# Moving the q, k transposes to the crossbar DMA and making x the stationary operand of the sequence mixer

## The chip, the cores and the metric

The kernel runs on one core of one Trainium2 chip. The metric is the device time of one execution in microseconds (us). Some executions are slower at a lower granted TensorE clock than others of the same kernel; here it was 4 of the 50 of the experiments' kernels, 1.5 to 2.0% above the mean of their kernel's fast ones, at a clock of 0.962 to 0.974 against 0.968 to 0.982. Such runs are marked slow and are left out of every ratio (the medians below are over all runs). Engines are named as the profile names them: PE is TensorE's matmuls, PEld its weight loads, DVE is VectorE, ACT is ScalarE, POOL is GpSimd, and SP is SyncE, whose queue (SPq) issues DMAs. `L246` is line 246 of the kernel in question.

## The reference, cut to what matters

```python
# q, k, v: (8 batches, 8 heads, 576, 64), s: (8, 8, 576)
scores = q @ k.T / 8 + min(-(cum[i] - cum[j]), 0)   # cum = cumsum(max(s, 0)); causal
x = softmax(scores) @ v                             # heads side by side: (8, 576, 512)
u = x + (x.T @ U @ V).T                             # sequence mixer: U (576, 32), V (32, 576)
out = u + relu(u @ w_ch1) @ w_ch2                   # channel mixer, 512 -> 2048 -> 512
```

## The kernel before

The 64 heads are worked in 32 pairs, four pairs to a batch. The channel mixer of finished batches (`chanmix`, 9 groups) is cut into small steps. They fill TensorE between the steps of the attention (`step_fill`). The parts that the change and the argument touch:

```python
def load_qk(b, h, n):                       # GpSimd's queue, f32 -> bf16
    for dst, src in ((q_t[b], q), (k_t[b], k)):
        nc.gpsimd.dma_start(out=dst[:, ds(h, n), :], in_=...)     # 72 partitions x (8 rows x 64)

def transposes(n):                          # of pair n
    ...                                     # SP: cum rows of the pair into the slot
    for hh in range(2):
        tp = pwork()...                     # a PSUM buffer, one of 4
        for c, src in enumerate((q_t[b], k_t[b])):
            for t2 in range(4):
                nc.tensor.transpose(tp[:, c, t2, :], src[:, h, ds(t2 * 128, 128)], identity[:TP, :TP])
        for par in range(2):
            copy = nc.scalar.copy if n == 0 or (b == 1 and par) else nc.vector.tensor_copy
            copy(dst[:, :, :, :, par], tp[par * D : par * D + D]...)      # into the pair's slot
        yield

def seqmix(b):
    for t in range(5):                      # x U, with U padded to 128 columns as stationary operand
        nc.tensor.matmul(up, lhsT=U_sb[:, t, :], rhs=x_sb[:, :, t, :], ...)      # 512 columns move
    nc.vector.tensor_copy(ux, up)
    yield
    ...                                     # u = x + V-part, 512 columns per matmul

for n in range(PB, NP + 2):                 # the second stage: pairs 4 to 31 (PB = 4, NP = 32)
    b, hp = divmod(n, PB)
    if hp == 0 and 1 < b < B - 1:
        load(b + 1)
    if n + 1 < NP:
        run(transposes(n + 1))              # run(): after each yield, one step of chanmix
    if n < NP:
        run(scores(n))
    ...                                     # seqmix of the batch before, values(n - 1)
in_program_order(tc, traced, [E.Pool, E.PE])
```

Each engine then works through its own list in that order; the traces below show DVE standing 6.36 and 16.72 us at one instruction while a later one is ready.

Names: a slot is the buffer from which a pair's scores are computed (transposed q and k, and the cum rows); there are five, and pair n uses slot n mod 5. `pwork` is a PSUM buffer that matmuls write. `x_sb` is x, the attention's result, as DVE writes it after dividing by the softmax's sum; `ux` is x U; `o_sb` is a piece of the output. `xT` and `u_sd` are transposed by the crossbar DMA (DMA_TRANSPOSE on SP's queue) in this kernel already.

Lines named below: L237 transposes of q and k, L243 copies into the slots, L321 values, L349 x U, L385 and L408 V, L432 and L444 the two channel-mixer matmuls, L98 q, k loads. In the changed kernel the same are L246, L254, L332, L361, L404 and L427, L451 and L463, L97; L342 writes x_sb, L473 writes o_sb, L222 is the new crossbar transpose, which writes `qkT`.

The softmax here doesn't subtract the row's maximum and nothing guards it: scores larger than these inputs give would overflow.

Of the kernel before, what the change touches and what calls it, by code (L numbers as in the profile page):

```python
# [13 lines left out]
BF16 = mybir.dt.bfloat16  # L14
# [25 lines left out]
def kernel(  # L40
# [12 lines left out]
    nc = tc.nc  # L53
    traced = len(nc.cur_bb.bb.instructions)
    E = mybir.EngineType
    B, H, S, D = q.shape
    assert (B, H, S, D) == (8, 8, 576, 64)
    DM = H * D
    FF = 4 * DM
    R = moe_U.shape[1]  # L60
    scale = 1.0 / (D ** 0.5)
    BH = B * H
    NP = BH // 2
    PB = NP // B
    TP, TT = 72, 8
    NG = B * S // 512
    KA = D + 4
    NF = FF // 128
    FT = 2

    consts = ctx.enter_context(tc.tile_pool(name="consts", bufs=1))
    loads = ctx.enter_context(tc.tile_pool(name="loads", bufs=2))
    work = ctx.enter_context(tc.tile_pool(name="work", bufs=2))
    ps_s = ctx.enter_context(tc.tile_pool(name="ps_s", bufs=4, space=bass.MemoryType.PSUM))
    ps_w = ctx.enter_context(tc.tile_pool(name="ps_w", bufs=4, space=bass.MemoryType.PSUM))
# [4 lines left out]
    def pwork():  # L80
        return ps_w.tile([128, 512], FP32, tag="w", name="pwork")
# [5 lines left out]
    rows = s_early[:BH, : 8 * S].rearrange("p (r c s) -> p r c s", r=4, c=2)  # L87
    nc.sync.dma_start(out=s_sb, in_=s.rearrange("b h s -> (b h) s"))

    q_t, k_t = {}, {}  # L90

    def alloc_qk(b):
        q_t[b] = loads.tile([TP, H, TT * D], BF16, tag="q_sd", name="q_sd")
        k_t[b] = loads.tile([TP, H, TT * D], BF16, tag="k_sd", name="k_sd")

    def load_qk(b, h, n):
        for dst, src in ((q_t[b], q), (k_t[b], k)):  # L97
            nc.gpsimd.dma_start(  # L98
                out=dst[:, ds(h, n), :],
                in_=src[b, ds(h, n)].rearrange("h (p t) d -> p h (t d)", p=TP),  # L100
            )

    alloc_qk(0)
    load_qk(0, 0, 2)
    identity = consts.tile([128, 128], BF16)
    make_identity(nc, identity)
# [5 lines left out]
        out=keep,  # L112
        in_=keep,
# [49 lines left out]
    for n in range(PB):  # L163
        for hh in range(2):
            nc.sync.dma_start(
                out=slots[n][D:KA, hh, 0 : 2 * S],
                in_=rows[2 * n + hh : 2 * n + hh + 1].rearrange("n r c s -> n r (c s)"),
            )

    for dst in (q_t[0], k_t[0]):  # L170
        nc.vector.memset(dst[:, 4:8, 0:2], 0.0)
    load_qk(0, 4, 4)
    init_v(nc.vector, v_slots[0])
    for pT in pTs:
        nc.vector.memset(pT[:, :, 1600:], 1.0)
    U_sb = consts.tile([128, 5, 128], BF16)
    nc.vector.memset(U_sb, 0.0)
    V_sb = consts.tile([128, S], BF16)
    nc.vector.memset(V_sb, 0.0)
    rows_hbm = nc.dram_tensor("rows_hbm", (4, BH, 2, S), BF16, kind="Internal").ap()  # L180
    nc.sync.dma_start(
        out=rows_hbm[:, ds(2 * PB, BH - 2 * PB)].rearrange("r n c s -> n r c s"),
        in_=rows[2 * PB :],
    )

    def load_v(b):
# [13 lines left out]
    w1_sb = consts.tile([128, 4, FF], BF16)  # L200
    w2_sb = consts.tile([128, NF, DM], BF16)
    nc.gpsimd.dma_start(
        out=U_sb[:, :4, :R], in_=moe_U[:512].rearrange("(kt kp) r -> kp kt r", kp=128)
    )
    nc.gpsimd.dma_start(out=U_sb[:64, 4, :R], in_=moe_U[512:576])
    nc.gpsimd.dma_start(out=V_sb[:R], in_=moe_V)
    nc.gpsimd.dma_start(out=w1_sb, in_=moe_w_ch1.rearrange("(kt kp) n -> kp kt n", kp=128))
    nc.gpsimd.dma_start(out=w2_sb, in_=moe_w_ch2.rearrange("(kt kp) n -> kp kt n", kp=128))
    alloc_qk(1)
    load_qk(1, 0, H)  # L210
    load_v(1)

    uT_of, x_of, xT_of = {}, {}, {}

    def uT(g):
        if g not in uT_of:
# [1 line left out]
        return uT_of[g]  # L218



    def transposes(n):  # L222
        b, hp = divmod(n, PB)
        slot = slots[n % NSLOT]
        if b > 0:
            nc.sync.dma_start(
                out=slot[D:KA, :, 0 : 2 * S],
                in_=rows_hbm[:, ds(2 * n, 2)].rearrange("r n c s -> r n (c s)"),
            )
        for hh in range(2):  # L230
            h = 2 * hp + hh
            tp = pwork().bitcast(BF16)[:, : 2 * 4 * TP].rearrange(
                "p (c t m) -> p c t m", c=2, t=4
            )
            for c, src in enumerate((q_t[b], k_t[b])):
                for t2 in range(4):
                    nc.tensor.transpose(  # L237
                        tp[:, c, t2, :], src[:, h, ds(t2 * 128, 128)], identity[:TP, :TP]
                    )
            dst = slot[0:D, hh, 0 : 2 * S].rearrange("p (c m t two) -> p c m t two", c=2, t=4, two=2)  # L240
            for par in range(2):
                copy = nc.scalar.copy if n == 0 or (b == 1 and par) else nc.vector.tensor_copy
                copy(  # L243
                    dst[:, :, :, :, par],
                    tp[par * D : par * D + D].rearrange("p c t m -> p c m t"),
                )  # L246
            yield
# [61 lines left out]
    def values(n):  # L309
        b, hp = divmod(n, PB)  # L310
        if hp == 0:
            x_of[b] = work.tile([128, PB, 5, 128], BF16, tag="x_sb", name="x_sb")
            if b >= FT:
                xT_of[b] = work.tile([128, 4, 640], BF16, tag="xT", name="xT", bufs=1)
        x_sb, pT, vt = x_of[b], pTs[n % 2], v_slots[b % 3]
        for hh in range(2):
# [19 lines left out]
            )  # L336
            if hh == 1 and b >= FT:
                nc.sync.dma_start_transpose(
# [5 lines left out]

    def seqmix(b):
        x_sb = x_of.pop(b)
        up = pwork()
        for t in range(5):
            nc.tensor.matmul(  # L349
                up,  # L350
                lhsT=U_sb[:, t, :],
                rhs=x_sb[:, :, t, :],
                start=(t == 0),
                stop=(t == 4),
            )
        ux = work.tile([128, DM], BF16, tag="ux", name="ux")
        nc.vector.tensor_copy(ux, up)  # L357
        yield
        xT = xT_of.pop(b, None)
        cut = 512 - 64 * b  # L360

        def evac(dt, lo, hi, src):

            g, at = (b, 64 * b + lo) if lo < cut else (b + 1, lo - cut)
            dst = uT(g)[:, dt, at : at + hi - lo]
            if xT is not None:
                nc.vector.tensor_tensor(dst, src, xT[:, dt, lo:hi], op=ALU.add)  # L367
            elif b == 0 and type(dt) is int and dt % 2:
                nc.scalar.copy(dst, src)
            else:  # L370
                nc.vector.tensor_copy(dst, src)

        for dt in range(4):
            ut = pwork()
            if xT is None:
                for t in range(4):
                    nc.tensor.matmul(
                        ut[:, ds(t * 128, 128)],
                        lhsT=x_sb[:, dt, t, :],
                        rhs=identity,  # L380
                        start=(t == 0),
                        stop=False,
                        skip_group_check=True,
                    )
            nc.tensor.matmul(  # L385
                ut,
                lhsT=ux[:, ds(dt * 128, 128)],
                rhs=V_sb[:, 0:512],
                start=(xT is not None),
                stop=True,  # L390
                skip_group_check=True,
            )
            evac(dt, 0, cut, ut[:, 0:cut])
            if cut < 512:
                evac(dt, cut, 512, ut[:, cut:512])
            yield
        ut = pwork()[:, 0:256].rearrange("p (a b) -> p a b", a=4)
        for dt in range(4):
            if xT is None:
                nc.tensor.matmul(  # L400
                    ut[:, dt, :],
                    lhsT=x_sb[:, dt, 4, :],
                    rhs=identity[:, :64],
                    start=True,  # L404
                    stop=False,
                    skip_group_check=True,
                )
            nc.tensor.matmul(  # L408
                ut[:, dt, :],
                lhsT=ux[:, ds(dt * 128, 128)],  # L410
                rhs=V_sb[:, 512:S],
                start=(xT is not None),
                stop=True,
                skip_group_check=True,
            )
        evac(slice(0, 4), 512, S, ut)
        yield
# [59 lines left out]
    def run(gen):  # L477
        for _ in gen:
            step_fill()

    def drain(gen):
        for _ in gen:
            pass
# [10 lines left out]
    for n in range(PB):  # L494
        drain(scores(n, 1))
        if n + 2 < PB:
            drain(transposes(n + 2))
        if n > 0:
            drain(values(n - 1))
    drain(values(PB - 1))  # L500
    spin(4, pscore)
    for _ in seqmix(0):
# [2 lines left out]


    def load(b):
        alloc_qk(b)
        load_qk(b, 0, H)
        load_v(b)  # L510

# [3 lines left out]
    fill_with(14)  # L515
    pace[1] = 3
    run(transposes(PB))
    for n in range(PB, NP + 2):
        b, hp = divmod(n, PB)
        if hp == 0 and 1 < b < B - 1:  # L520
            load(b + 1)
        if n + 1 < NP:
            run(transposes(n + 1))
        if n < NP:
            run(scores(n))
        if hp == 1 and b > FT:
            run(seqmix(b - 1))
            fill.append(chanmix(b - 1))
        if PB < n <= NP:
            run(values(n - 1))  # L530
            if hp == 0 and b <= FT:
                run(seqmix(b - 1))
                fill.append(chanmix(b - 1))
                pace[1] = 7
# [35 lines left out]
```

## Time and profile before

The median of three runs was 401.76 us. The profiled run took 402.07 us.

| part | value | view |
|---|---|---|
| PE busy | 95% of 400.4 us, granted clock 0.983 | page |
| DVE, ACT busy | 56%, 50% | page |
| PE share of the chain of waits | 76% | page |
| q, k transposes | 512 matmuls of 72 columns | groups |

The table of stages of the kernel before: after the stretch come its length, then busy us (and instructions) of PE, PEld, DVE, ACT and POOL, then PE's granted clock, the DMA share (as the tool prints it; it can exceed 1) and GB/s.

```profile
80.00:100.00 20.00, 18.09 (x180) 10.70 (x177) 15.08 (x33) 8.85 (x19) 0.69 (x1) 1.00 1.26 116
100.00:120.00 20.00, 20.00 (x216) 11.95 (x214) 12.70 (x27) 12.92 (x26) 5.88 (x7) 1.00 1.17 106
120.00:140.00 20.00, 18.61 (x183) 10.53 (x182) 15.86 (x35) 7.41 (x15) 0.00 (x0) 1.00 0.43 77
140.00:160.00 20.00, 20.00 (x209) 11.88 (x208) 12.74 (x25) 14.74 (x29) 5.88 (x7) 1.00 1.49 135
160.00:180.00 20.00, 20.00 (x184) 11.23 (x182) 14.32 (x30) 6.85 (x14) 0.00 (x0) 1.00 0.28 57
```

PE is full or nearly so; no other engine is. In this part PE issue time is span. What the removed work costs PE is read from the timeline, from the start of one row to the start of the next (the second column is the time from the first start to the last end, which overlaps the next row):

```profile
199.94 0.29 PE L237 MATMUL pwork<-identity,q_sd 72*128 72x72 bf16 x4
200.07 0.29 PE L237 MATMUL pwork<-identity,k_sd 72*128 72x72 bf16 x4
200.19 1.03 PE L444 MATMUL pwork<-w_sb,hT 128*128 128x512 bf16 x4
...
214.78 1.24 PE L349 MATMUL pwork<-x_sb,U_sb 128*128 128x512 bf16 x5
```

Eight transposes take 0.25 us. The five x U matmuls take about 5 x 0.215 = 1.08 us.

### The profile page before, as it was taken

How to read it: one execution, taken by the hardware profiler on the slowest of the kernel's cores; microseconds unless marked ns; L12 is line 12 of the kernel's file. 1: busy time of each engine (PE TensorE's matmuls, PEld its weight loads, DVE VectorE, ACT ScalarE, POOL GpSimd, SP SyncE). 2: the span in 40 equal slices, each digit the busy share in tenths (PEclk: the TensorE clock that was granted, in tenths of full speed). 3: DMA queues.
4: the chain of work that ended last, by engine and by line, in shares of the span. 5: the costliest groups of instructions: out<-in, count | busy, mean ns of one | idle time of the engine just before them, and what ended most of it. 6: DMA issues, size and time to landing. Idle time of an engine off the chain costs nothing.

```text
span 400.4 us, 8275 instructions
## 1 busy us (share of the span) xinstructions
PE 381.6 (95%) x3395; PEld 213.8 (53%) x3395; DVE 223.8 (56%) x473; ACT 200.5 (50%) x384; POOL 56.6 (14%) x79
## 2 busy tenths in 40 slices
PE   7798989989999899999999999999999999999995
PEld 2475446645655455555554566555555554444442
DVE  7775036777567866776676756775668252002011
ACT  5552578735753477336743584348533920630610
POOL 5760052300500050005000500000000000000000
PEclk9759999999999999999999999999999999999999
DMA  5999999994596299319951792240154015301002
GB/s 76 160 213 207 166 121 141 137 146 85 82 133 86 67 148 120 55 56 175 114 67 57 141 145 54 72 97 18 38 77 97 16 34 133 79 26 71 10 26 79
DMA packets 94148, 38.31 MB, mean 96 GB/s; under 512 B 77150, under 2 KB 88446, under 8 KB 94110
## 3 DMA queue, kind: packets, MB, share of 16 engines
q0 software_dynamic: 53360, 18.44, 57.5%
q1 hardware_dynamic: 40750, 19.35, 24.1%
q8 instruction: 26, 0.43, 0.5%
q14 instruction: 12, 0.10, 0.1%
HBM read 37.51 MB, written 9.95 MB: 119 GB/s over the span
## 4 chain that ended last, share of the span: by engine, by line
PE 76%; DMA 11%; DVE 6%; ACT 3%; issue 1%; POOL 1%; DVEq 0%; ACTq 0%
PE pwork L444 28%; PE pwork L432 28%; PE pscore L258 8%; DMA k_sd<-in_k_dram 8%; PE pwork L321 6%; PE pwork L237 3%; DMA v_slot_102<-in_v_dram 2%; PE pwork L349 2%; PE pwork L385 2%; DVE slot_96 L243 1%; DVE slot_95 L243 1%; DMA hT<-in_s_dram 1%; DVE x_sb L331 1%; DVE ux L357 1%; DVE o_sb L454 1%
## 5 line engine op out<-in xcount | busy, mean ns | idle before, releaser
L439 ACT ACTIVATE hT<-pwork 128x512 bf16<-128x512 f32 x144 | 88.0, 611 | 112.5 <-PE pwork L432 111.6
L444 PE MATMUL pwork<-w_sb,hT 128*128 128x512 bf16 x576 | 141.3, 379 | 0.2 <-ACT slot_96 L243 0.2
L432 PE MATMUL pwork<-uT,w_sb 128*128 128x512 bf16 x576 | 141.0, 379 | 0.4 <-ACT slot_96 L243 0.3
L444 PEld LDWEIGHTS <-hT 128*128 128x128 bf16 x576 | 52.3, 98 | 50.1 <-issue 0.3
L432 PEld LDWEIGHTS <-w_sb 128*128 128x128 bf16 x576 | 51.0, 98 | 46.9 <-issue 0.4
L454 DVE TENSOR_TENSOR o_sb<-pwork,u_sd 128x512 f32<-128x512 f32 x36 | 24.9, 692 | 63.4 <-PE pwork L444 62.2
L269 ACT ACTIVATE pT_87<-pscore 128x512 bf16<-128x512 f32 x32 | 19.3, 604 | 28.3 <-PE pscore L258 28.2
L331 DVE TENSOR_TENSOR x_sb<-pwork,rec 128x320 bf16<-128x320 f32 x64 | 31.3, 490 | 2.0
L98 POOL DMA_DIRECT2D q_sd<-in_q_dram x10 | 8.3, 829 | 148.6 <-PE pwork L237 132.5
L269 ACT ACTIVATE pT_86<-pscore 128x512 bf16<-128x512 f32 x32 | 19.3, 604 | 18.5 <-PE pscore L258 18.4
L243 DVE COPY slot_96<-pwork 64x576 bf16<-64x576 bf16 x22 | 17.4, 797 | 13.8 <-PE pwork L237 13.5
L270 DVE TENSOR_TENSOR pT_86<-pT_86,keep 128x512 bf16<-128x512 bf16 x32 | 13.2, 414 | 21.1 <-ACT pT_86 L269 21.0
L330 DVE RECIPROCAL rec<-pwork 128x5 f32<-128x5 f32 x64 | 12.1, 191 | 20.8 <-PE pwork L321 20.7
L367 DVE TENSOR_TENSOR uT<-pwork,xT 128x256 bf16<-128x256 f32 (+6 forms) x54 | 19.8, 418 | 6.1 <-PE pwork L385 6.1
L270 DVE TENSOR_TENSOR pT_87<-pT_87,keep 128x512 bf16<-128x512 bf16 x32 | 13.2, 417 | 17.5 <-ACT pT_87 L269 17.4
L237 PEld LDWEIGHTS <-q_sd 72*128 72x128 bf16 x256 | 15.9, 100 | 12.8 <-DMA q_sd<-in_q_dram 1.6
L237 PE MATMUL pwork<-identity,k_sd 72*128 72x72 bf16 x256 | 19.1, 201 | 2.9 <-DMA k_sd<-in_k_dram 2.8
L243 DVE COPY slot_93<-pwork 64x576 bf16<-64x576 bf16 x26 | 20.7, 798 | 2.2 <-PE pwork L237 1.9
L282 ACT ACTIVATE pT_87<-pscore 128x512 bf16<-128x512 f32 x32 | 19.5, 610 | 4.6 <-PE pscore L258 4.5
L282 ACT ACTIVATE pT_86<-pscore 128x512 bf16<-128x512 f32 x32 | 19.5, 609 | 4.5 <-PE pscore L258 4.5
L321 PEld LDWEIGHTS <-pT_87 128*128 128x128 bf16 x480 | 18.6, 99 | 5.8 <-DVE pT_87 L295 0.4
L321 PEld LDWEIGHTS <-pT_86 128*128 128x128 bf16 x480 | 18.4, 100 | 4.8 <-DVE uT L367 0.5
(96 smaller groups left out, 434.1 us busy)
## 6 DMA issues: line engine op xcount, KB each, us to landing
out_dram<-o_sb SPq DMA_DIRECT2D x36, 256.0 KB
w_sb<-in_moe_w_ch_dram POOLq DMA_DIRECT2D x2, 2048.0 KB, 20.6
q_sd<-in_q_dram POOLq DMA_DIRECT2D x7, 576.0 KB, 8.1
k_sd<-in_k_dram POOLq DMA_DIRECT2D x7, 576.0 KB, 14.0
v_slot_102<-in_v_dram POOLq DMA_DIRECT2D x12, 128.0 KB, 14.3
v_slot_103<-in_v_dram POOLq DMA_DIRECT2D x12, 128.0 KB, 14.7
v_slot_104<-in_v_dram POOLq DMA_DIRECT2D x8, 128.0 KB, 16.9
rows_hbm<-hT SPq DMA_DIRECT2D x1, 504.0 KB
```

Of the source, the lines that this page charges most:

```text
L237: nc.tensor.transpose(tp[:, c, t2, :], src[:, h, ds(t2 * 128, 128)], identity[:TP, :TP])
L243: copy(dst[:, :, :, :, par], tp[par * D : par * D + D].rearrange("p c t m -> p c m t"),)
L258: nc.tensor.matmul(dst, lhsT=kT[:, ds(j * 128, 128)], rhs=qT[:, lo:hi], start=True, stop=True,)
L269: nc.scalar.activation(pT[:, hh, 0:512], diag, EXP, scale=scale)
L270: nc.vector.tensor_tensor(pT[:, hh, 0:512].rearrange("p (a b) -> p a b", a=4), pT[:, hh, 0:512].rearrange("p (a b) -> p a b", a=4), keep.t ...
L282: nc.scalar.activation(pT[:, hh, 512:1024], far, EXP, scale=scale)
L321: nc.tensor.matmul(po[:, i, :], lhsT=pT[:, hh, ds(place(j, i), 128)], rhs=vt[:, j, h, :], start=(j == 0), stop=(j == i), skip_group_check= ...
L331: nc.vector.tensor_tensor(x_sb[:, hp, :, ds(hh * D, D)], po[:, :, 0:D], rec.to_broadcast([128, 5, D]), op=ALU.mult,)
L432: nc.tensor.matmul(f1, lhsT=w1_sb[:, kt, ds(nf * 128, 128)], rhs=u[:, kt, :], start=(kt == 0), stop=(kt == 3),)
L439: nc.scalar.activation(hT[:, nf, :], f1, RELU)
L444: nc.tensor.matmul(f2, lhsT=hT[:, nf, ds(i * 128, 128)], rhs=w2_sb[:, nf, :], start=(nf == 0), stop=(nf == NF - 1),)
L454: nc.vector.tensor_tensor(o_sb.rearrange("p (a b) -> p a b", a=4), f2.rearrange("p (a b) -> p a b", a=4), u_sd[:, :, i, :], op=ALU.add,)
```

## The change

The intent is to take work off the full engine in two places. First, q and k of batches 3 to 7 are transposed by the crossbar DMA, issued from SP two pairs ahead, instead of by PE. Second, x U is computed with x as stationary operand and only U's 32 columns moving. The result comes out transposed, so one more matmul against the identity turns it back. V is kept in four copies, each at its own 32 rows, so that the stacked result can be used directly.

```diff
+    QT = 3
+    TR = 80
+    qks = [consts.tile([TR, H, 2, TT * D], BF16, name=f"qk{i}") for i in range(2)]
...
+    def fetch(n):
+        b, hp = divmod(n, PB)
+        qkT_of[n] = work.tile([128, 2, 2, 4, TR], BF16, tag="qkT", name="qkT")
+        nc.sync.dma_start_transpose(
+            out=qkT_of[n].rearrange("p a c t m -> p (a c t) m"),
+            in_=qks[b % 2][:, ds(2 * hp, 2), :, :].rearrange("p h c x -> p (h c x)"),
+        )
...  in transposes(n)
+            if qkT is not None:
+                tp = qkT[:, hh, :, :, :TP]          # no PE, no PSUM; the copies follow as before
+            else:
...  in seqmix(b)
-        for t in range(5):
-            nc.tensor.matmul(up, lhsT=U_sb[:, t, :], rhs=x_sb[:, :, t, :], ...)
-        ux = work.tile([128, DM], BF16, tag="ux", name="ux")
+        for dt in range(4):
+            for t in range(5):
+                nc.tensor.matmul(up[:, ds(dt * R, R)], lhsT=x_sb[:, dt, t, :], rhs=U_sb[:, t, :], ...)
+        uxT = work.tile([128, 128], BF16, tag="uxT", name="uxT")
+        nc.vector.tensor_copy(uxT, up)
+        yield
+        up = pwork()[:, 0:128]
+        nc.tensor.matmul(up, lhsT=uxT, rhs=identity, start=True, stop=True)
+        ux = work.tile([128, 128], BF16, tag="ux", name="ux")
...  before the last values of the first stage
+    for dt in range(1, 4):
+        nc.vector.tensor_copy(V_sb[ds(dt * R, R), dt, :], V_sb[:R, 0, :])
...  in load(b): the 80-row transpose also reads 8 pad rows, so they are cleared first
+        if QT <= b < QT + 2:
+            nc.gpsimd.memset(qks[b % 2][64:, :, :, :], 0.0)
...  in the loop over pairs, ahead of transposes(n + 1)
+        if QT * PB <= n + 2 < NP:
+            fetch(n + 2)
```

More of the change, by code (lines that the diff above doesn't have):

```diff
@@ L60 @@
     R = moe_U.shape[1]
+    assert R == 32
     scale = 1.0 / (D ** 0.5)
@@ L69 @@
     FT = 2
+    QT = 3
     consts = ctx.enter_context(tc.tile_pool(name="consts", bufs=1))
-    loads = ctx.enter_context(tc.tile_pool(name="loads", bufs=2))
     work = ctx.enter_context(tc.tile_pool(name="work", bufs=2))
@@ L88 @@
     nc.sync.dma_start(out=s_sb, in_=s.rearrange("b h s -> (b h) s"))
-    q_t, k_t = {}, {}
-    def alloc_qk(b):
-        q_t[b] = loads.tile([TP, H, TT * D], BF16, tag="q_sd", name="q_sd")
-        k_t[b] = loads.tile([TP, H, TT * D], BF16, tag="k_sd", name="k_sd")
+    TR = 80
+    qks = [consts.tile([TR, H, 2, TT * D], BF16, name=f"qk{i}") for i in range(2)]
     def load_qk(b, h, n):
-        for dst, src in ((q_t[b], q), (k_t[b], k)):
+        for c, src in enumerate((q, k)):
             nc.gpsimd.dma_start(
-                out=dst[:, ds(h, n), :],
+                out=qks[b % 2][:TP, ds(h, n), c, :],
                 in_=src[b, ds(h, n)].rearrange("h (p t) d -> p h (t d)", p=TP),
             )
-    alloc_qk(0)
     load_qk(0, 0, 2)
@@ L168 @@
             )
-    for dst in (q_t[0], k_t[0]):
-        nc.vector.memset(dst[:, 4:8, 0:2], 0.0)
+    nc.vector.memset(qks[0][:TP, 4:8, :, 0:2], 0.0)
     load_qk(0, 4, 4)
@@ L175 @@
         nc.vector.memset(pT[:, :, 1600:], 1.0)
-    U_sb = consts.tile([128, 5, 128], BF16)
-    nc.vector.memset(U_sb, 0.0)
-    V_sb = consts.tile([128, S], BF16)
+    U_sb = consts.tile([128, 5, R], BF16)
+    nc.vector.memset(U_sb[64:, 4, :], 0.0)
+    V_sb = consts.tile([128, 4, S], BF16)
     nc.vector.memset(V_sb, 0.0)
@@ L202 @@
     nc.gpsimd.dma_start(
-        out=U_sb[:, :4, :R], in_=moe_U[:512].rearrange("(kt kp) r -> kp kt r", kp=128)
+        out=U_sb[:, :4, :], in_=moe_U[:512].rearrange("(kt kp) r -> kp kt r", kp=128)
     )
-    nc.gpsimd.dma_start(out=U_sb[:64, 4, :R], in_=moe_U[512:576])
-    nc.gpsimd.dma_start(out=V_sb[:R], in_=moe_V)
+    nc.gpsimd.dma_start(out=U_sb[:64, 4, :], in_=moe_U[512:576])
+    nc.gpsimd.dma_start(out=V_sb[:R, 0, :], in_=moe_V)
     nc.gpsimd.dma_start(out=w1_sb, in_=moe_w_ch1.rearrange("(kt kp) n -> kp kt n", kp=128))
     nc.gpsimd.dma_start(out=w2_sb, in_=moe_w_ch2.rearrange("(kt kp) n -> kp kt n", kp=128))
-    alloc_qk(1)
     load_qk(1, 0, H)
     load_v(1)
-    uT_of, x_of, xT_of = {}, {}, {}
+    uT_of, x_of, xT_of, qkT_of = {}, {}, {}, {}
     def uT(g):
@@ L229, in transposes @@
             )
+        qkT = qkT_of.pop(n, None)
         for hh in range(2):
             h = 2 * hp + hh
-            tp = pwork().bitcast(BF16)[:, : 2 * 4 * TP].rearrange(
-                "p (c t m) -> p c t m", c=2, t=4
-            )
-            for c, src in enumerate((q_t[b], k_t[b])):
-                for t2 in range(4):
-                    nc.tensor.transpose(
-                        tp[:, c, t2, :], src[:, h, ds(t2 * 128, 128)], identity[:TP, :TP]
-                    )
+            if qkT is not None:
+                tp = qkT[:, hh, :, :, :TP]
+            else:
+                tp = pwork().bitcast(BF16)[:, : 2 * 4 * TP].rearrange(
+                    "p (c t m) -> p c t m", c=2, t=4
+                )
+                for c in range(2):
+                    for t2 in range(4):
+                        nc.tensor.transpose(
+                            tp[:, c, t2, :],
+                            qks[b % 2][:TP, h, c, ds(t2 * 128, 128)],
+                            identity[:TP, :TP],
+                        )
             dst = slot[0:D, hh, 0 : 2 * S].rearrange("p (c m t two) -> p c m t two", c=2, t=4, two=2)
@@ L346, in seqmix @@
         x_sb = x_of.pop(b)
-        up = pwork()
-        for t in range(5):
-            nc.tensor.matmul(
-                up,
-                lhsT=U_sb[:, t, :],
-                rhs=x_sb[:, :, t, :],
-                start=(t == 0),
-                stop=(t == 4),
-            )
-        ux = work.tile([128, DM], BF16, tag="ux", name="ux")
+        up = pwork()[:, 0:128]
+        for dt in range(4):
+            for t in range(5):
+                nc.tensor.matmul(
+                    up[:, ds(dt * R, R)],
+                    lhsT=x_sb[:, dt, t, :],
+                    rhs=U_sb[:, t, :],
+                    start=(t == 0),
+                    stop=(t == 4),
+                    skip_group_check=True,
+                )
+        uxT = work.tile([128, 128], BF16, tag="uxT", name="uxT")
+        nc.vector.tensor_copy(uxT, up)
+        yield
+        up = pwork()[:, 0:128]
+        nc.tensor.matmul(up, lhsT=uxT, rhs=identity, start=True, stop=True)
+        ux = work.tile([128, 128], BF16, tag="ux", name="ux")
         nc.vector.tensor_copy(ux, up)
@@ L386, in seqmix @@
                 ut,
-                lhsT=ux[:, ds(dt * 128, 128)],
-                rhs=V_sb[:, 0:512],
+                lhsT=ux,
+                rhs=V_sb[:, dt, 0:512],
                 start=(xT is not None),
@@ L409, in seqmix @@
                 ut[:, dt, :],
-                lhsT=ux[:, ds(dt * 128, 128)],
-                rhs=V_sb[:, 512:S],
+                lhsT=ux,
+                rhs=V_sb[:, dt, 512:S],
                 start=(xT is not None),
@@ L507, in load @@
     def load(b):
-        alloc_qk(b)
+        if QT <= b < QT + 2:
+            nc.gpsimd.memset(qks[b % 2][64:, :, :, :], 0.0)
         load_qk(b, 0, H)
```

## The prediction

> **What bounds it.** TensorE. In the table of stages it is busy about 20 of 20 us in nearly every stage from 100 to 380 us at granted clock 1.00; VectorE has 12 to 16 us, ScalarE 7 to 15. The waits view finds almost no TensorE idle then (DVE ux 2.1 us in all). The chain of waits is 76% PE. So a microsecond of TensorE issue time is a microsecond of span. Mean matmul durations overlap; I use start-to-start times from the timeline.
>
> **What the change removes from TensorE.**
> 1. Transposes of q, k for batches 3 to 7: 40 heads x 8. Timeline at 199.94 us: eight start in 0.25 us. 40 x 0.25 = 10.1 us.
> 2. Mixer, x U: five 512-column matmuls, 1.08 us per batch (timeline at 214.8 us), become 20 of 32 columns, each with its own weight load. Neighbours of 64 and 65 columns with loads start every 28 to 30 ns here[...]. Estimate 27 ns x 20 = 0.54 us, plus 0.06 us for the new transposing matmul: 0.45 us saved per batch, 3.2 us over the seven batches in the busy part.
>
> **What it adds or moves.**
> - 20 crossbar transposes on SP. The same kind holds SP's queue 1.2 us (128x640) and 1.9 to 2.2 us (128x2048) here; estimate 2 us each, fetched two pairs (about 18 us) ahead. Off the path.[...]
> - GpSimd clears of the pad before loads 3 and 4: about 6 us each from its memsets here, for loads needed over 20 us later. Off the path.
> - DVE's slot copies of batches 3 to 7 read SBUF instead of PSUM: 798 ns now[...]. DVE doesn't bind.
> - Start: V's larger clear (+0.65 us DVE, absorbed by waits for k), three copies of V[...], in seqmix(0) one more round trip and two more spins, against shorter matmuls and casts. Net 0 to +0.7 us, plus or minus 1.5 because the clock falls to 0.5 to 0.8 at 16 to 29 us and may fall elsewhere.
> - The ux wait (0.8 us at most) splits into two shorter ones.
>
> **Sum.** -10.1 - 3.2 + 0.4 = -12.9: 401.8 becomes about 388.8 us; range 385 to 393.5. Chances: faster by over 2% 0.87, within 2% 0.12, slower 0.01.
>
> **What would show it.** Transposes 512 -> 192; pairs from batch 3 on start 8.3 to 8.4 us apart instead of 8.9; U matmuls of a batch start within 0.55 us; TensorE still full from 100 us;[...] SP transposes near 2 us, nobody waiting long for qkT.
>
> **What would make it wrong.** 32-column matmuls bound by their 128-column weight loads ([...]the mixer gains nothing, about 392 us); copies or transposes late, so scores wait; SP held at a transpose waiting for its load, delaying slot rows, stores or xT; pad clears pushing q, k or v of batches 3 and 4 late; the framework making q's and k's loads wait for each other in their shared tile; a worse start or clock dip.

The forecast's sum came to -12.9 us (-10.1 - 3.2 + 0.4). The 27 ns for a 32-column matmul is the author's estimate, somewhat below the 28 to 30 ns measured at 64 and 65 columns; with 28 to 30 ns the saving is 0.42 to 0.46 us per batch (1.08 less 20 of them, less 0.06), 2.9 to 3.2 us over seven batches. So the -3.2 can be had from the trace as well. The 0.06 us is near the 55 ns between the starts of 128-column matmuls (kernel before, from 201.06 us). The +0.4 is the estimate for the start; the three copies of V in the changed kernel each took 0.30 us. The +0.65 us follows from the clears of V and U in the kernel before, 0.30 and 0.33 us: three more of the first, most of the second saved. The 6 us for a pad clear follows from GpSimd's memsets of 128 and 520 columns, 0.24 and 0.53 us, or 0.74 ns a column for 8,192 columns.

## More of the kernel before

The framework orders each engine's instructions itself, at compile time, unless the kernel pins them. In the first stage (pairs 0 to 3) the kernel pins DVE, ACT and SP. Over the whole kernel it pins only GpSimd and TensorE. In the second stage DVE, ACT and SP run in the order that the compile-time scheduler chose.

The slot copies, in the groups view by shape (busy us and mean ns, then DVE's idle time before them and who ended it):

```profile
L243 DVE COPY slot_93<-pwork 64x576 bf16<-64x576 bf16 x26 | 20.7, 798 | 2.2 <-PE pwork L237 1.9
```

Here each copy is released by the transpose just ahead of it on PE, whose order is pinned. So the copies come in turn, 7 to 18 us ahead of their pair's scores (pairs 8 to 31). Those of pairs 11 to 13 on DVE's timeline:

```profile
102.06 3.26 DVE L243 COPY slot_93<-pwork 64x576 bf16<-64x576 bf16 x4 [0.40 <-PE pwork L237]
110.92 3.26 DVE L243 COPY slot_94<-pwork 64x576 bf16<-64x576 bf16 x4 [0.40 <-PE pwork L237]
119.79 3.26 DVE L243 COPY slot_95<-pwork 64x576 bf16<-64x576 bf16 x4 [0.27 <-PE pwork L237]
```

GpSimd issues batch 4's loads as soon as the last transpose that reads the buffer is done:

```profile
103.31 0.84 POOL L98 DMA_DIRECT2D q_sd<-in_q_dram  x1 [22.59 <-PE pwork L237]
```

## The result, and the profile after

The change made the kernel slower. The median of its runs was 427.74 us (427.64 to 430.83; one more run, of 427.03 us), against 402.68 us before. The ratio was 1.063 (95% interval 1.0573 to 1.0688). Ratios in this document are the mean time of one kernel's fast runs over the mean of the other's in the same rounds, so they are not quite the ratio of the medians.

The same stages after, for the profiled run (430.83 us, 3 us longer than the others):

```profile
80.00:100.00 20.00, 11.48 (x149) 7.34 (x146) 11.84 (x26) 6.86 (x14) 3.62 (x5) 0.76 1.96 148
100.00:120.00 20.00, 19.50 (x176) 11.31 (x177) 19.30 (x39) 9.51 (x19) 2.54 (x1) 0.92 0.50 88
120.00:140.00 20.00, 16.78 (x132) 8.71 (x130) 11.46 (x18) 8.95 (x19) 12.56 (x10) 0.83 1.22 92
140.00:160.00 20.00, 7.79 (x74) 4.40 (x73) 2.91 (x5) 3.54 (x7) 4.23 (x5) 0.77 1.86 128
160.00:180.00 20.00, 14.89 (x107) 7.76 (x107) 14.21 (x35) 4.80 (x10) 1.66 (x2) 0.71 1.30 157
```

PE has holes in 80 to 100 and in 140 to 180 us, and the other engines have them too. So the engines wait for each other. The granted clock falls beside the holes: from 1.00 to 0.50 at 92.9 us, 1.5 us after PE had stopped, and at 79.3 us, 1.2 us after the end of a hole of 1.66 us. After the 15.27 us hole below, at 0.50, four 512-column matmuls take 1.86 us instead of 1.03. Over the whole span PE is busy 381.6 us in both kernels although it has less to do after. Part of that time ran at a lower clock (mean 0.926 instead of 0.983); the repaired kernel found below has the same matmuls and is busy 369.7 us at 0.978. Whether the clock makes up all of these 12 us was not worked out.

When each pair's first exp starts shows where the time goes (read from the traces; the last row is the repaired kernel found below):

| start, us | pair 8 | 12 | 13 | 14 | 16 | 31 | last matmul ends |
|---|---|---|---|---|---|---|---|
| before | 81.2 | 122.0 | 130.9 | 143.3 | 160.9 | 315.9 | 395.9 |
| after | 87.2 | 140.6 | 165.4 | 181.3 | 197.7 | 345.2 | 425.4 |
| repaired | 83.6 | 121.6 | 130.0 | 142.4 | 158.8 | 304.8 | 385.0 |

The changed kernel loses 38 us up to pair 14 (181.3 - 143.3). After pair 16 it runs as predicted: pairs within a batch start 8.1 to 8.4 us apart instead of 8.6 to 8.9, and the stretch from pair 16 to 31 takes 147.5 us instead of 155.0. So the saving is there, and the loss at the changeover is five times the 7.5 us saved in that stretch.

What stood still? PE's timeline of the changed kernel (in brackets: idle time before the row, and what ended it):

```profile
90.84 0.53 PE L361 MATMUL pwork<-U_sb,x_sb 128*128 128x32 bf16 x15
99.23 0.31 PE L361 MATMUL pwork<-U_sb,x_sb 128*128 128x32 bf16 x5 [7.87 <-DVE x_sb L342]
...
163.06 1.86 PE L463 MATMUL pwork<-w_sb,hT 128*128 128x512 bf16 x4 [15.27 <-DVE o_sb L473]
```

PE waits for DVE, for x_sb and for o_sb. DVE's timeline over the same time says why (slot_91 at 98 us is the slot of pair 12, slot_89 at 108 us that of pair 10, slot_90 at 156 us that of pair 16):

```profile
91.59 0.19 DVE L341 RECIPROCAL rec<-pwork 128x5 f32<-128x5 f32 x1
98.14 0.65 DVE L254 COPY slot_91<-qkT 64x576 bf16<-64x576 bf16 x1 [6.36 <-DMA qkT<-qk_70]
98.71 0.47 DVE L342 TENSOR_TENSOR x_sb<-pwork,rec 128x320 bf16<-128x320 f32 x1
...
108.07 3.27 DVE L254 COPY slot_89<-pwork 64x576 bf16<-64x576 bf16 x4
...
156.20 1.97 DVE L254 COPY slot_90<-qkT 64x576 bf16<-64x576 bf16 x3 [16.72 <-DMA qkT<-qk_69]
...
162.32 0.69 DVE L473 TENSOR_TENSOR o_sb<-pwork,u_sd 128x512 f32<-128x512 f32 x1
```

At 91.8 us DVE has computed a reciprocal, and the x_sb product that PE waits for is ready to run. In front of it in DVE's list stands a copy for pair 12, whose scores start only at 140.6 us. Its qkT has not landed. DVE stands 6.36 us at that copy and PE stands behind DVE. At 139.5 us the same happens for 16.72 us with a copy for pair 16, whose scores start at 197.7 us. Copies of pairs 12 and 13 ran before those of pair 10, and those of pair 14 before those of pair 11. In the kernel before, all pairs were copied in turn. Two crossbar transposes, for pairs 16 and 17, hold SP's queue during the second stand:

```profile
138.31 14.34 SPq L222 DMA_TRANSPOSE qkT<-qk_69  x2
```

The loads are late as well. GpSimd's timeline of the changed kernel around batch 4's load, and one DVE row beside it:

```profile
117.46 6.92 POOL L530 MEMSET qk_69<- 16x8192 bf16 x1 [31.91 <-PE pwork L246]
124.68 1.13 POOL L97 DMA_DIRECT2D qk_69<-in_q_dram  x1 [0.30 <-POOL qk_69 L530]
```

```profile
119.81 5.63 DVE L254 COPY slot_89<-qkT 64x576 bf16<-64x576 bf16 x2
```

Batch 4's load goes out at 124.7 us instead of 103.3: part of this is the delay that PE already had at pair 11, and 6.9 us of it is the pad clear. The first of the two copies in the DVE row took 4,971 ns (others 656) and ended 0.4 us after the clear did. It is a copy for pair 15, whose scores start at 189.6 us; an x_sb product stands behind it, and PE waits 3.2 us for that. The three holes of PE (7.9, 3.2 and 15.3 us) make 26 of the 38 us; the rest was not taken apart.

### The profile page after: what moved, and what is told of

It is laid out like the page before. It is cut to its first block, busy times and chain, and to the rows that moved or that the text cites. A ratio compares the mean times of both kernels' runs of the same rounds, so it can differ in the third digit from the quotient of the medians.

```text
span 429.1 us, 7959 instructions
## 1 busy us (share of the span) xinstructions
PE 381.6 (89%) x3205; PEld 211.0 (49%) x3205; DVE 215.0 (50%) x483; ACT 201.2 (47%) x384; POOL 70.9 (17%) x81
## 3 DMA queue, kind: packets, MB, share of 16 engines
q1 hardware_dynamic: 66990, 25.90, 34.4%
## 4 chain that ended last, share of the span: by engine, by line
PE 57%; DMA 24%; issue 9%; DVE 5%; POOL 5%; ACT 0%; POOLq 0%; DVEq 0%; ACTq 0%
PE pwork L451 23%; PE pwork L463 22%; DMA v_slot_100<-in_v_dram 12%; PE pscore L269 6%; PE pwork L332 5%; DMA v_slot_101<-in_v_dram 4%; DMA qkT<-qk_69 4%; DMA v_slot_99<-in_v_dram 2%; POOL qk_69 L530 2%; DVE o_sb L473 2%; POOL v_slot_100 L189 1%; POOL qk_69 L97 1%; PE pwork L404 1%; DMA hT<-in_s_dram 1%; POOL v_slot_99 L189 1%
## 5 line engine op out<-in xcount | busy, mean ns | idle before, releaser
L463 PE MATMUL pwork<-w_sb,hT 128*128 128x512 bf16 x576 | 143.7, 388 | 15.4 <-DVE o_sb L473 15.3
L463 PEld LDWEIGHTS <-hT 128*128 128x128 bf16 x576 | 54.0, 100 | 70.4 <-issue 19.5
L451 PEld LDWEIGHTS <-w_sb 128*128 128x128 bf16 x576 | 52.3, 99 | 56.4 <-DVE x_sb L342 3.9
L280 ACT ACTIVATE pT_84<-pscore 128x512 bf16<-128x512 f32 x32 | 19.3, 603 | 45.7 <-PE pscore L269 45.5
L280 ACT ACTIVATE pT_83<-pscore 128x512 bf16<-128x512 f32 x32 | 19.3, 603 | 17.1 <-PE pscore L269 17.0
L332 PEld LDWEIGHTS <-pT_83 128*128 128x128 bf16 x480 | 19.5, 101 | 7.4 <-issue 2.4
L293 ACT ACTIVATE pT_84<-pscore 128x512 bf16<-128x512 f32 x32 | 19.5, 610 | 7.3 <-PE pscore L269 7.3
L386 DVE TENSOR_TENSOR uT<-pwork,xT 128x256 bf16<-128x256 f32 (+6 forms) x54 | 19.4, 418 | 6.4 <-PE pwork L404 6.4
L293 ACT ACTIVATE pT_83<-pscore 128x512 bf16<-128x512 f32 x32 | 19.5, 610 | 4.7 <-PE pscore L269 4.6
L332 PEld LDWEIGHTS <-pT_84 128*128 128x128 bf16 x480 | 18.8, 100 | 5.3 <-DVE pT_84 L306 0.3
L254 DVE COPY slot_90<-qkT 64x576 bf16<-64x576 bf16 x16 | 10.5, 655 | 19.7 <-DMA qkT<-qk_69 16.7
L148 PE MATMUL pscore<-busy 128*128 128x512 bf16 (+1 forms) x53 | 18.9, 449 | 1.3 <-DVE busy L124 1.3
L297 ACT ACTIVATE pT_83<-pscore 128x512 bf16<-128x512 f32 x32 | 19.7, 616 | 0.0
L297 ACT ACTIVATE pT_84<-pscore 128x512 bf16<-128x512 f32 x32 | 19.7, 614 | 0.0
L254 DVE COPY slot_89<-qkT 64x576 bf16<-64x576 bf16 x16 | 14.8, 928 | 3.5 <-PE pscore L269 3.3
```

Source lines behind the costliest of these rows:

```text
L254: copy(dst[:, :, :, :, par], tp[par * D : par * D + D].rearrange("p c t m -> p c m t"),)
L280: nc.scalar.activation(pT[:, hh, 0:512], diag, EXP, scale=scale)
L293: nc.scalar.activation(pT[:, hh, 512:1024], far, EXP, scale=scale)
L297: nc.scalar.activation(pT[:, hh, 1024:1536], mid, EXP, scale=scale)
L332: nc.tensor.matmul(po[:, i, :], lhsT=pT[:, hh, ds(place(j, i), 128)], rhs=vt[:, j, h, :], start=(j == 0), stop=(j == i), skip_group_check= ...
L451: nc.tensor.matmul(f1, lhsT=w1_sb[:, kt, ds(nf * 128, 128)], rhs=u[:, kt, :], start=(kt == 0), stop=(kt == 3),)
```

## The experiments

Twelve experiments ran, on three chips; each has its own runs of the kernel before, which its experiments share. The scheduler gives each kernel an order of its own. Theory 1: DVE's order, in which slot copies overtook more urgent work, is the cause. Theory 2: the pad clears on GpSimd hold the loads. Theory 3: crossbar transposes are slow in themselves, up to 9.1 us of SP's queue. A further rival was the mixer's new round trip.

| label | kernel | median us, all runs | ratio of fast runs (95%) |
|---|---|---|---|
| - | the change | 427.74 | 1.063 (1.0573 to 1.0688) |
| e1_dve_order | change, DVE in program order throughout | 400.88 | 0.9907 (0.9835 to 0.9979) |
| e1b_before_dve_order | before, DVE in program order throughout | 407.47 | 1.011 (1.0076 to 1.0143) |
| e3_qk_only | crossbar part alone | 428.79 | 1.0626 (1.0584 to 1.0667) |
| e4_mix_only | mixer part alone | 401.46 | 0.9951 (0.991 to 0.9991) |
| e2_pad_dma | change, pads by DMA | 428.08 | 1.0637 (1.0583 to 1.0691) |
| e6_clear_dve10 | change, DVE in order from pair 10 | 395.93 | 0.9814 (0.976 to 0.9867) |
| e7_pad_dve10 | both | 390.43 | 0.9691 (0.9645 to 0.9737) |
| e8_pad_dve10_sp10 | both, and SP in order | 432.12 | 1.071 (1.0653 to 1.0766) |
| e9_best_no_mix | e7 without the mixer part | 392.12 | 0.9724 (0.9688 to 0.9759) |
| e10_pin_copies | pads by DMA, only the copies pinned | 391.41 | 0.9696 (0.9658 to 0.9735) |
| e11_best_qt2 | e7, crossbar from batch 2 on | 403.17 | 1.000 (0.9946 to 1.0055) |
| e12_best_again | e7 again, 5 rounds | 390.45 | 0.9693 (0.9655 to 0.9731) |

All gave correct results.

### Which part, and is it the order?

e1 pins DVE in the changed kernel; e1b does the same in the kernel before:

```diff
-    in_program_order(tc, traced, [E.Pool, E.PE])
+    in_program_order(tc, traced, [E.Pool, E.PE, E.DVE])
```

> The changed kernel with VectorE's instructions kept in program order to the end (before, only the first stage was; the compile-time scheduler ordered the rest). Theory 1, VectorE's order: the scheduler put slot copies of later pairs ahead of work that TensorE needs first, VectorE then stood 6.4 and 16.7 us at copies whose qkT had not landed, and TensorE 7.9 and 15.3 us behind it. Then this run falls to 389 to 395 us, VectorE's waits for qkT come to under 2 us in all and TensorE is full from 100 us. Theory 2, the pad clears of GpSimd (6.9 us each) hold the loads: the clears are still here, so the time stays above 410 us. Theory 3, the crossbar transposes are slow in themselves (up to 9.1 us on SP's queue): also above 410 us.

> The kernel before with the same line changed: VectorE in program order to the end. Theory 1 says that order matters only where copies can run ahead, which copies from PSUM cannot by much (four buffers), so 399 to 404 us, the same as before. If it comes out near 390 us, the order is a gain of its own, and e1 must be read against it.

e3 puts the old `seqmix`, U and V back; e4 keeps the new mixer and sends all batches through PE (`QT = 8`).

> The crossbar part alone, the sequence mixer as before. All three theories put the loss in the crossbar part: 425 to 438 us. The prediction's sum would make it 392 us; a rival, that the mixer's new round trip (uxT, ux) exposes waits that did the harm, would make it 390 to 395 us too.

> The mixer part alone: q and k through TensorE in all batches (in the shared tile). The prediction's sum: 398 to 399.5 us (-3.2 us of TensorE time, +0.4 at the start). If 32-column matmuls are bound by their weight loads[...] it stays at 401 to 403 us; if the shared tile made the loads of q and k wait for each other, 405 us or more.

e3 is as slow as the whole change, and e4 is 0.5% faster than before. The loss lies in the crossbar part, and the rival about the mixer falls. e1 wins back 27 us with one word, so theory 3 by itself falls: the transposes are still there. But its fast runs took 396.5 to 402.1 us, all above the 389 to 395 that theory 1 expected, so something else was left. e1b gives one piece of it: pinning DVE everywhere costs the kernel before 1.1%, which I had not expected. Its stages show where: PE is busy 16.38 us in 60 to 80 us and 16.32 in 80 to 100, against 18.85 and 18.09 before. The scheduler's order is better than the program's there, and worse where the crossbar begins. What makes it better was not examined.

### Order and clears, apart and together

e2 fills the pad rows (which nobody uses) by two small DMAs instead of the clear, at the same place:

```diff
-            nc.gpsimd.memset(qks[b % 2][64:, :, :, :], 0.0)
+            for c, src in enumerate((q, k)):
+                nc.gpsimd.dma_start(
+                    out=qks[b % 2][TP:, :, c, :],
+                    in_=src[b, :, 0:64].rearrange("h (p t) d -> p h (t d)", p=TR - TP),
+                )
```

e6 pins DVE only from the iteration where the first transpose is fetched:

```diff
+        if n == QT * PB - 2:
+            mark = len(nc.cur_bb.bb.instructions)
...
+    in_program_order(tc, mark, [E.DVE])
```

e7 does both, and e8 pins SP too (`[E.DVE, E.SP]`).

> The changed kernel, its two pad clears on GpSimd (6.9 us each) replaced at the same place by two small DMAs each that fill the pad rows with 64 rows of q and k (nobody reads the pad's columns). VectorE's order is still the scheduler's. If the clears were the main cause (theory 2): 390 to 400 us. If VectorE's order is (theory 1): loads come some 6 us sooner, the two waits for qkT shrink by about that much each, 410 to 422 us.

> The changed kernel with VectorE in program order only from pair 10 on, where the first transpose is fetched; the stage before it keeps the scheduler's order, which the run of the kernel before in program order showed to be worth 1.1%. Clears still on GpSimd. Expected: the 401 us of the run in program order throughout, less about 4 us: 395 to 398 us.

> Both: pads by DMA and VectorE in program order from pair 10 on. In the run with program order throughout TensorE still stood 4 us in 140 to 180 us behind a copy that waited 7.5 us for qkT of batch 4, whose load had stood behind a clear. If that was the clear: 388 to 392 us, the prediction's sum, with waits for qkT under 2 us. If the crossbar transposes are late for another reason (they share the DMA engines with the loads, and are wanted two pairs sooner than the TensorE transposes were), it stays at 394 us or more.

That transposes and loads share the DMA engines is on the pages of the two kernels: with the 20 transposes SP's queue (q1) grew by 26,240 packets, from 24.1% to 34.4% of the 16 engines' span, beside 57.0% for the loads' queue (q0) in the changed kernel.

> As the run before, and SP's queue in program order from pair 10 on too, so that no transpose is issued ahead of stores and slot rows that stand before it in the program. If SP's order matters: 1 to 4 us less than the run before; if not, within 1 us of it; if SP then stands at a fetch whose load has not landed, slower.

e2 alone changes nothing: 428 us, where theory 1 had allowed 410 to 422 and theory 2 under 400. Batch 3's q and k did land sooner, at 85.0 us instead of 93.1. But in e2's order DVE came to the first such copy at 80 us instead of 92 and stood 12.6 us at it. With that delay batch 4's loads went out no sooner than in the change (124.1 against 124.7 us), and DVE stood 19.4 us at the next. The waits of e2 and of e7 for qkT:

```profile
DVE slot L254 <- DMA qkT<-qk: 32.0, 2, 19.4
DVE slot L254 <- DMA qkT<-qk: 4.8, 3, 2.0
```

e6 gives 395.9 and e7 390.4 us. Once the order is right, the clears cost 1.2% (0.9814 - 0.9691), about 5 us. Here theory 2 is the second cause, and it can be seen only after the first is gone. e7 is within 2 us of the prediction's 388.8; its copies still waited 4.8 us for qkT (three times, 2.0 us at the longest), where I had expected under 2.

e8 missed what I had hoped for. The waits view of e8 (who waited for what: us in total, times, longest):

```profile
DVE slot L254 <- DMA qkT<-qk: 36.2, 4, 11.5
PE pscore L269 <- DMA slot<-rows_hbm: 31.1, 4, 9.6
```

In program order on SP, the fetches and the slot's cum rows come late, and PE and DVE wait for them. SP's own queue waits 88.4 us for o_sb at its stores, and 47.8 us for x_sb and 27.9 us for slot copies at its xT transposes. So it stands at a store or an xT that is not ready, with the fetch that DVE needs behind it. That is the same fault as on DVE, on another queue. That each of these waits feeds the next is argued from the trace, not shown by a run.

### How narrow is the cause, and what is each part worth?

e10 leaves DVE to the scheduler but holds each copy from qkT behind the DVE instruction that precedes it in the program:

```diff
+                seen = len(nc.cur_bb.bb.instructions)
                 copy = nc.scalar.copy if n == 0 or (b == 1 and par) else nc.vector.tensor_copy
                 copy(...)
+                if qkT is not None:
+                    after_the_last(tc, seen, E.DVE)   # an order-only dependency, no semaphore
```

e9 is e7 with the old mixer. e11 is e7 with `QT = 2`. e12 is e7 once more.

> Pads by DMA; VectorE's order left to the scheduler but for one thing: each slot copy that reads qkT is held behind the VectorE instruction that precedes it in the program. If the copies' overtaking is the cause (theory 1, in its narrow form): 388 to 396 us. If some other reordering on VectorE did the harm: above 405 us.

> The crossbar part repaired (pads by DMA, VectorE in program order from pair 10 on), with the sequence mixer as in the kernel before. The repaired whole took 390.4 us. If the mixer part is worth what the prediction took for it (3.2 us of TensorE time less 0.4 at the start): 393 to 394 us. If as little as the mixer-only run showed (0.5%): 392 us.

> The repaired kernel with the crossbar from batch 2 on. TensorE has 64 transposes less, worth 2 us: 388 us if the prefetch is in time. But batch 2 is loaded at 46 to 70 us[...], and its first transpose is wanted at about 60 us. If deadlines of the loads decide, copies wait for qkT by more than 3 us and it takes 392 to 402 us.

> The repaired kernel again, as the base for the other three and for its number: 388.5 to 391.5 us, ratio 0.967 to 0.972.

e10 gives 391.4 us. Its control is e2, which differs from it in this hold alone: the ratio to the kernel before falls from 1.0637 to 0.9696. Holding back 80 copies is enough, so the cause is their overtaking; no other reordering on DVE is needed to explain the loss. The waits view of e10:

```profile
DVE slot L270 <- DMA qkT<-qk: 6.6, 3, 2.5
```

e9 against e12 puts the mixer at 0.3% (1.2 us) on top of the repaired crossbar, and e4 put it at 0.5% (2.0 us); the prediction took 2.8. The intervals of e9 and e12 overlap, so the 1.2 is rough. The traces, one run each, show more: from the first exp of pair 4 to that of pair 31 it takes 253.3 us in e4 against 256.5 before, and 244.4 in e12 against 247.3 in e9, so 3.2 and 2.9 us less. In e4 pair 4 starts 0.7 us later than before (60.1 against 59.4). The repaired crossbar alone is worth 2.8% (11 us), against 10.1 predicted.

e11 loses all of it again, although PE has 64 transposes fewer. Its waits view:

```profile
DVE slot L254 <- DMA qkT<-qk: 23.5, 8, 4.5
PE pwork L361 <- DVE o_sb L473: 6.3, 1, 6.3
```

Batch 2's first fetches go out at 71.7 and 73.1 us, while pair 8's scores started at 81.2 us in the kernel before. Even in program order DVE now stands at copies eight times. So here the transposing DMA paid from batch 3 on (0.9693, e12) and not from batch 2 on (1.000, e11).

The repaired kernel, e12, in the same stages as above:

```profile
80.00:100.00 20.00, 18.26 (x225) 11.73 (x223) 16.73 (x39) 9.32 (x21) 0.78 (x2) 1.00 1.94 160
100.00:120.00 20.00, 20.00 (x208) 11.83 (x207) 11.90 (x27) 14.25 (x29) 5.87 (x7) 1.00 1.15 105
120.00:140.00 20.00, 18.62 (x181) 10.48 (x179) 16.01 (x38) 7.67 (x15) 6.17 (x7) 1.00 1.23 149
140.00:160.00 20.00, 20.00 (x176) 11.29 (x175) 12.00 (x27) 15.75 (x32) 0.00 (x0) 1.00 1.50 146
160.00:180.00 20.00, 19.72 (x182) 10.95 (x181) 14.98 (x36) 6.79 (x15) 6.59 (x7) 1.00 0.99 131
```

PE is as full as before at full clock, and batch 4's load goes out at 104.8 us. This version beats both kernels: 390.45 us, 3.1% faster than before and 8.7% faster than the change as it was made (390.45 / 427.74, a ratio of medians). It was run at another time.

## Why the prediction was wrong, point by point

- **PE is the bound, and PE's savings are span.** Right for the steady part and for the repaired kernel: -12.9 us predicted net; 0.9693 of 402.98 us, or -12.4 us, measured in e12. That the sum comes so close is in part luck: in the means the crossbar gave 0.9 us more than forecast and the mixer 0.8 to 1.6 us less. In the changed kernel PE stopped being the bound between 90 and 180 us.
- **Transposes, -10.1 us.** Right: 512 became 192, pairs are 8.1 to 8.4 us apart (forecast 8.3 to 8.4), and e9 gained 11 us.
- **x U, -3.2 us in the busy part, +0.4 at the start.** Right in mechanism, somewhat too large: the first to the last start of the 20 32-column matmuls is 0.48 us, so 25.2 ns from one to the next against my 27. The mixer part measured 1.2 to 2.0 us as a mean. In the single traces above its two terms came out as predicted (2.9 to 3.2 us less after pair 4, 0.7 us more before it in e4), so the shortfall of the mean may be noise; this was not settled.
- **"20 crossbar transposes on SP ... Off the path."** This is the step that failed. I checked that the transposes were short and fetched about two pairs early, not who would stand in line at their completion. The copies no longer hung on PE, whose order is pinned, but only on a DMA and a free slot. In the compile-time order they moved 42 to 70 us ahead of their use (pair 12: copy at 98.1 us, scores at 140.6; pair 14: 111.6 and 181.3), against 7 to 18 us in the kernel before, and in front of x_sb and o_sb. DVE stood 6.36 and 16.72 us at them, and PE 7.87 and 15.27 us behind DVE. That the new freedom is why the scheduler moved them is argued from the two programs; e10 shows that holding them back repairs it. I listed "copies or transposes late, so scores wait" as a risk. What happened was different: the scores of those pairs were far off, and other work waited behind the copies.
- **"GpSimd clears ... Off the path."** Wrong in effect, close in size: 6.9 us each against my 6. With the order repaired they cost about 5 us (e6 against e7). Counting two pairs of lead as slack was the error, because those pairs move the deadline of the load forward by the same amount.
- **Transposes near 2 us.** In the changed kernel 14 of the 20 held SP 1.3 to 1.4 us, but the longest 9.15. I took 1.9 to 2.2 us from the kernel before and left out its one transpose of 8.0 us (u_sd at 41.0 us). The longest ran from 143.5 us in the changed kernel; what sets the spread was not tested. By itself this did not cause the loss: e7 has transposes of up to 6.3 us.
- **Copies from SBUF.** The forecast's figures for them were the author's estimate; they were too low. Measured: 656 ns (798 from PSUM). It cost nothing: DVE is busy 11.9 to 16.7 of 20 us in the stages of the repaired kernel above.
- **The risk of SP held at a transpose** did not decide the change itself but is real: pinning SP's order brought it on (e8).
- **Chances.** I gave slower by over 2% one in a hundred. The sum was sound and the order of the queues was not part of it; that chance was far too small for a change that replaces what releases 80 instructions.

## What to carry to other kernels

When an operation is moved from a pinned engine to a DMA, ask what used to hold its consumers in place: an instruction that now waits only for a DMA can be scheduled early, and the work behind it in its engine's list waits as well (here DVE stood 6.36 and 16.72 us at such copies, with x_sb and o_sb behind them). After such a change read, on each engine, which instruction stands at the head during each hole and when its result is needed; if that is tens of us later (here 42 us for pair 12's copy), pin it to program order there, and only there. A prefetch distance is also a deadline for the load in front of it, so look at what delays that load before calling a clear or a transfer off the path (here two clears of 6.9 us cost about 5 us).
